# Loading the values by head pair, planning VectorE's and GpSimd's shared port, and filling TensorE's planned gaps in the opening with unread products

## The chip, the cores and the metric

The kernel runs on one core of a Trainium2 chip. The metric is the time of one execution on the device in microseconds; of several runs the median counts. Of the engines, TensorE (PE in the profile) multiplies, VectorE (DVE), ScalarE (ACT) and GpSimd (POOL) do the rest, and SyncE (SP) issues most of the transfers from the chip's memory.

## What is computed

Attention in a causal band of 64 positions for 8 batches of 8 heads (576 positions of 64 numbers), then a feed-forward layer on the 4608 tokens:

```python
scores = matmul(q, k.T) / 8; scores = where((rel >= 0) & (rel < 64), scores, -1e9)
attn = exp(scores - max); attn = attn / (sum(attn) + 1e-9)
x = matmul(attn, v)               # 4608 x 512, the heads side by side
h = x @ w_in                      # 512 x 2048
g = maximum(h, 0) + alpha * minimum(h, 0)
out = g @ w_out                   # 2048 x 512
```

All of it is in float32. The weights come as 64-bit floats, which the kernel turns into two parts itself.

## The kernel before

**Tiles and blocks.** The tokens are cut into 36 tiles of 128 (`t`), four tiles make a block (nine blocks), and the 2048 hidden features are cut into 16 groups of 128 (`f`). For each tile, `attend` loads q, k and v, multiplies scores (`score`, L366), adds the mask and takes the row's extreme on DVE (L382), the exponential on ACT (L388), the reciprocal of the sum on DVE (L399, L400), scales on POOL (L404), transposes the weights, and multiplies with v (`value`, L457). Tiles 0 to 7 are transposed on PE (`turn`, L421, and a copy `put`, L426 or L428), the others on DVE (L442). The result x is kept in a high part (`xh`, ACT, L461) and a low part (`xl`, DVE, L464), so that three products of a faster kind, high with high, low with high and high with low, stand for one in full float32.

**The feed-forward layer.** A `cell` is one block and one `f`: 12 products for h (L497), a slope on ACT (L503) and a maximum on DVE (L506), the high part `gh` on ACT (L511), the low part `gl` on POOL or, in block 0, on POOL or DVE (L515), and 12 products into the output (L530). The first four `f` of block 0 are done in two halves, tiles 0 and 1, then 2 and 3, with 256 columns instead of 512.

**The weights.** All 32 pieces (16 of w_in, 16 of w_out, in turn) are loaded into three `raw` buffers and converted once, by `weights`, while blocks 0 and 1 run: `two` (ACT or DVE, L260, L262), `shift` (DVE, L267, L270), `low` (ACT, L275), `val` (DVE, L279), the sum (POOL, L283), the high part `win_h` or `wout_h` (ACT, L298) and the low part `win_l` or `wout_l` (POOL or DVE, L302).

**The order.** All steps go into a `Plan` with their engines, a hold time and a latency each, written by hand in microseconds, with buffers taken and given and with due times. `order` (L73) walks through them like a list scheduler: it picks the step that can begin first on an engine, and among those within 0.12 us the one that is due first; where a step names two engines it takes the better. The sorted start times then give the order in which instructions are issued, once, when the program is built. On the chip, each engine runs its own instructions in that order and waits for what they need. PSUM's eight banks are split: 0 to 3 are kind `o` (the output sums of a block; before those begin, the first two tiles' scores and transposes and the first weights' `two`), 4 to 7 kind `bank`. A transposed weight tile lies in `pt`; the DVE path relies on zeros in the parts that it does not write, so a second such tile is set to zero by POOL (`birth`, L600).

**Loads.** q and k are one DMA each a tile. v of a tile lies as 128 rows (two overlapping stretches of 64 positions, each with the next) and is loaded in two DMAs of 64 partitions each (L346). For tiles 0 and 1 the second is issued from ACT's queue, all else from SP's. At most eight loads are in flight in the plan.

Of the kernel before, what the change touches and what calls it, by code (L numbers as in the profile page):

```python
# [24 lines left out]
FLIGHT = 8  # L25
SWITCH = 0.11
# [9 lines left out]
class Step:  # L36
    def __init__(self, engines, emit, after, behind, take, give, want, moved):
        self.engines, self.emit, self.after = engines, emit, [a for a in after if a is not None]
        self.behind, self.take, self.give, self.want, self.moved = behind, take, give, want, moved
        self.before, self.tiled, self.next = [], False, None  # L40
        self.start = self.end = None
        self.late = math.inf


class Plan:
# [5 lines left out]
    def step(self, engines, emit, after=(), behind=(), take=(), give=(), want=math.inf, moved=0.0):  # L51

        s = Step(engines, emit, after, list(behind), list(take), list(give), want, moved)
        for a in s.after + s.behind:
            a.before.append(s)
        self.steps.append(s)
        return s
# [13 lines left out]
    def order(self):  # L73
        self.deadlines()
        free = {PE: 0.0, DVE: 0.0, ACT: 0.8, POOL: 3.6, SP: 0.8}
# [4 lines left out]
        while ready:  # L80
            best = None
            picks = {}
            for s in ready:
# [11 lines left out]
                for e, (hold, lat) in s.engines.items():  # L95
                    picks.setdefault(e, []).append((max(t0, free[e]), s, e))
# [8 lines left out]
            while s:  # L105
# [6 lines left out]
                free[e] = t + hold  # L112
                s.end = t + lat
# [24 lines left out]
        return sorted(done, key=lambda s: s.start)  # L138
# [16 lines left out]
def banded_attention_then_prelu_ffn(  # L155
# [58 lines left out]
    def weight(name, f):  # L214
# [6 lines left out]
    stock = dict(bank=[4, 5, 6, 7], o=[0, 1, 2, 3], q=["q0", "q1"], k=["k0", "k1"], v=["v0"], w=["w0", "w1"],  # L221
                 pt=["pt0"], new=[], g=["g0", "g1"], gh=["gh0", "gh1", "gh2"], gl=["gl0", "gl1"],
# [5 lines left out]
    plan = Plan(stock)  # L228
    step = plan.step
# [11 lines left out]
    def weights(c):  # L241
# [58 lines left out]
        def rest(e):  # L300
# [13 lines left out]
        s7 = step({POOL: (1.22, 1.28), DVE: (1.15, 1.22)}, rest, [s6], prior[1:] if prior[0] else [],  # L314
                  take=late("_l"), give=[val])
# [6 lines left out]
    def attend(t, by_pe, want, loads_behind=(), behind=(), last=None):  # L322
# [3 lines left out]
        wb, pb = Buffer("w", 2 if by_pe else 1), Buffer("pt", 1)  # L326
# [3 lines left out]
        def load_q(e):  # L330
            d["q"] = room(qb, [P, 2, 2 * P], F32, f"q_{t}")
            (nc.scalar if e == ACT else nc.sync).dma_start(
                d["q"], qT[:, :, t].rearrange("(y x) d h q -> (x d) y (h q)", x=2))

        def load_k(_):
# [3 lines left out]
        loads = [step({SP: (0.62, 0.62)}, load_q, (), loads_behind, take=[qb], moved=0.75),  # L339
                 step({SP: (0.62, 0.62)}, load_k, (), loads_behind, take=[kb], moved=1.05)]  # L340
        lv = []
        for u in range(2):
            def load_v(e, u=u):
                if u == 0:
                    d["v"] = room(vb, [P, NP, 2, P], F32, f"v_{t}")
                (nc.scalar if e == ACT else nc.sync).dma_start(  # L346
                    d["v"][u * W:(u + 1) * W].rearrange("w c b d -> w c (b d)"),
                    vN[:, :, 2 * t + u:2 * t + u + 2].rearrange("c w b d -> w c (b d)"))
            lv.append(step({ACT if t < 2 and u else SP: (0.62, 0.62)}, load_v, (), [*loads_behind, *lv[:1]],
                           take=[vb] if u == 0 else [], moved=0.8 if t < 2 else 1.2))  # L350
# [18 lines left out]
        cold = 1.0 + 0.9 * (t < 2)  # L369
# [5 lines left out]
        for u in range(2):  # L375
            some = []
            for e in range(NP):
                g = u * NP + e

                def mask(_, u=u, e=e, g=g):  # L380
                    m = masks[:, 1 if (t * P + u * W) % seq == 0 else 0, :]
                    nc.vector.tensor_tensor_reduce(  # L382
                        out=d["w"][:, g, :], in0=d["s"][e % 2][:, u, e // 2], in1=m, op0=ALU.add, op1=ALU.min,
# [11 lines left out]
        def norm(u0, u1, after):  # L395
# [11 lines left out]
            r = step({DVE: (0.33, 0.4)}, recip, after)  # L407
# [3 lines left out]
        if by_pe:  # L411
            for u in range(2):
# [17 lines left out]
                tr = step({PE: (0.37 * cold, 0.5 * cold)}, turn, [sc] + ready[-1:], take=[tb] + [pb] * (u == 0), give=[wb])  # L430
# [245 lines left out]
```

## Time and profile before

| | before |
|---|---|
| median of 3 runs | 920.72 us (919.67 to 922.1) |
| profiled execution | 924.34 us, span 922.3 us |
| mean granted clock of TensorE | 0.996 |
| PE busy | 894.2 us, 97% |
| DVE, ACT, POOL busy | 446.5, 382.9, 316.0 us |
| read, written | 59.25 MB, 9.44 MB |

The span goes from the first to the last instruction of the core; the execution's own time lies 2.04 us above it. A row of the timeline has the start and the duration in microseconds, the engine, the line, the operation, what is written from what is read, the number of instructions run together, and in brackets how long the engine stood idle before and what ended that. Rows by operation have busy time, mean in ns, and idle time before with its releasers. Rows of stretches have, after the stretch and its length, the busy time of PE, PE's weight loads, DVE, ACT and POOL with the number of instructions, then the granted clock as a share of full speed, the share of the DMA engines, and GB/s. Numbers at names in the program's order are buffer numbers. Lines of the new kernel are higher than those of the old by 22 to 48, as the code has grown.

### The profile page before, as it was taken

What the parts mean: (1) busy time and instruction counts of PE and PEld (TensorE: products, weight loads), DVE (VectorE), ACT (ScalarE), POOL (GpSimd) and SP (SyncE); (2) the same over time, 40 slices, a digit from 0 to 9 for tenths busy, and PEclk for the clock granted to TensorE, in tenths of its full rate; (3) what the DMA queues carried; (4) which work ended last, traced back from release to release, by engine and by line L of the source; (5) the groups of instructions that cost most, each with busy time, mean ns of one, the idle gap of its engine ahead of it and who ended that gap; (6) DMA issues with size and microseconds to landing.
All of it is one profiled execution on the core that took longest, in us unless ns stands there. A gap on an engine that the chain in (4) does not pass through costs nothing.

```text
span 922.3 us, 15273 instructions
## 1 busy us (share of the span) xinstructions
PE 894.2 (97%) x5873; PEld 729.2 (79%) x5873; DVE 446.5 (48%) x1315; ACT 382.9 (42%) x1019; POOL 316.0 (34%) x244
## 2 busy tenths in 40 slices
PE   4799899999999999999999999999999999999998
PEld 3687678888888888888888888888888888888886
DVE  4889893744544445444544444445444444422111
ACT  4877784333433333333433343334333433322222
POOL 3677673322333223322233322333223322322221
PEclk9899999999999999999999999999999999999999
DMA  9476544011221123111211131113211221001001
GB/s 249 144 238 217 183 143 150 23 52 52 91 60 52 52 52 99 52 52 51 86 40 37 42 98 52 52 53 98 52 52 52 63 87 52 1 1 46 1 1 46
DMA packets 55209, 69.68 MB, mean 76 GB/s; under 512 B 3408, under 2 KB 48480, under 8 KB 55136
## 3 DMA queue, kind: packets, MB, share of 16 engines
q1 hardware_dynamic: 54560, 68.17, 25.1%
q8 instruction: 46, 0.75, 0.4%
q10 hardware_dynamic: 576, 0.53, 0.3%
q14 instruction: 27, 0.22, 0.1%
HBM read 59.25 MB, written 9.44 MB: 74 GB/s over the span
## 4 chain that ended last, share of the span: by engine, by line
PE 87%; DMA 4%; DVE 3%; ACT 2%; POOL 2%; issue 1%; SPq 0%; POOLq 0%; ACTq 0%; DVEq 0%
PE h L497 41%; PE o L530 39%; PE av L457 4%; PE s L366 3%; DMA raw<-w_out 2%; DMA raw<-w_in 1%; DMA q<-qT 1%; DMA v<-vN 1%; DVE val L279 1%; POOL val L283 1%; POOL wout_l L302 0%; DVE win_l L302 0%; ACT w L388 0%; POOL gl L515 0%; PE t L421 0%
## 5 line engine op out<-in xcount | busy, mean ns | idle before, releaser
L515 POOL TENSOR_TENSOR gl<-g,gh 128x512 fp32r<-128x512 f32 (+1 forms) x139 | 178.9, 1287 | 427.5 <-ACT gh L511 425.8
L506 DVE SCALAR_TENSOR_TENSOR g<-h,s_sb,g 128x512 f32<-128x512 f32 (+1 forms) x148 | 108.8, 735 | 293.8 <-ACT g L503 293.7
L503 ACT ACTIVATE g<-h,sa_sb 128x512 f32<-128x512 f32 (+1 forms) x148 | 100.2, 677 | 332.0 <-PE h L497 329.3
L530 PE MATMUL o<-wout_h,gh 128*128 128x512 f32 x576 | 226.8, 394 | 0.2 <-ACT gh L511 0.2
L530 PE MATMUL o<-wout_l,gh 128*128 128x512 f32 x576 | 226.2, 393 | 0.0
L497 PE MATMUL h<-xh,win_h 128*128 128x512 f32 (+1 forms) x592 | 160.8, 393 | 2.7 <-DVE val L279 2.7
L442 DVE STREAM_TRANSPOSE pt<-w 32x256 f32<-32x256 f32 x336 | 146.6, 436 | 30.9 <-POOL w L404 26.0
L530 PE MATMUL o<-wout_h,gl 128*128 128x512 f32 x576 | 160.7, 392 | 0.4 <-POOL gl L515 0.4
L497 PE MATMUL h<-xl,win_h 128*128 128x512 f32 (+1 forms) x592 | 156.1, 385 | 0.0
L497 PE MATMUL h<-xh,win_l 128*128 128x512 f32 (+1 forms) x592 | 155.6, 385 | 0.0
L388 ACT ACTIVATE w<-w,nm 128x128 f32<-128x128 f32 x288 | 112.1, 392 | 63.0 <-DVE nm L382 62.9
L511 ACT CAST gh<-g 128x512 fp32r<-128x512 f32 (+1 forms) x148 | 90.1, 609 | 111.3 <-DVE g L506 111.3
L497 PEld LDWEIGHTS h<-xl,win_h 128*128 128x128 f32 x592 | 109.9, 189 | 23.0
L530 PEld LDWEIGHTS o<-wout_h,gl 128*128 128x128 f32 x576 | 108.2, 188 | 25.0 <-POOL gl L515 0.8
L497 PEld LDWEIGHTS h<-xh,win_h 128*128 128x128 f32 x592 | 107.1, 189 | 26.4 <-ACT two L260 2.4
L497 PEld LDWEIGHTS h<-xh,win_l 128*128 128x128 f32 x592 | 110.0, 189 | 22.5
L530 PEld LDWEIGHTS o<-wout_h,gh 128*128 128x128 f32 x576 | 108.2, 188 | 24.3 <-ACT gh L511 0.6
L530 PEld LDWEIGHTS o<-wout_l,gh 128*128 128x128 f32 x576 | 108.2, 188 | 23.3
L404 POOL TENSOR_TENSOR w<-w,rc 128x1024 f32<-128x1024 f32 (+1 forms) x44 | 70.7, 1608 | 152.9 <-DVE rc L400 147.7
L382 DVE CUSTOM_DVE_ANT_0 w<-s,masks 128x128 f32<-128x128 f32 x288 | 63.9, 286 | 67.7 <-PE s L366 67.7
L388 ACT ACTIVATION_READ_ACCUMULATOR w<-w,nm 128x1 f32 x288 | 54.3, 189 | 0.0
L366 PE MATMUL s<-k,q 64*64 64x128 f32 x1152 | 43.1, 288 | 8.7 <-DMA q<-qT 6.1
(46 smaller groups left out, 458.6 us busy)
## 6 DMA issues: line engine op xcount, KB each, us to landing
v<-vN SPq DMA_DIRECT2D x70, 256.0 KB, 5.1
k<-kT SPq DMA_DIRECT2D x36, 384.0 KB, 3.9
q<-qT SPq DMA_DIRECT2D x36, 256.0 KB, 4.9
out<-os SPq DMA_DIRECT2D x36, 256.0 KB, 2.3
raw<-w_in SPq DMA_DIRECT2D x16, 512.0 KB, 4.4
raw<-w_out SPq DMA_DIRECT2D x16, 512.0 KB, 4.1
v<-vN ACTq DMA_DIRECT2D x2, 256.0 KB, 8.0
alpha_sb<-alpha ACTq DMA_DIRECT2D x1, 8.0 KB, 3.3
```

The source lines that it names most:

```text
L366: nc.tensor.matmul(d["s"][x][h * W:(h + 1) * W, u, y], q[r, y, h, u * W:(u + 1) * W], k[r, y, u:u + 2, h, :], start=True, stop=True)
L382: nc.vector.tensor_tensor_reduce(out=d["w"][:, g, :], in0=d["s"][e % 2][:, u, e // 2], in1=m, op0=ALU.add, op1=ALU.min, scale=-SCALE, scal ...
L388: nc.scalar.activation(w, w, AF.Exp, scale=-1.0, bias=d["nm"][:, g:g + 1], accum_out=d["sm"][:, g:g + 1])
L404: nc.gpsimd.tensor_tensor(out=w, in0=w, in1=d["rc"][:, g].unsqueeze(2).broadcast_to(list(w.shape)), op=ALU.mult)
L442: nc.vector.transpose(d["pt"][ks, :, r], d["w"][r, :, ks])
L457: nc.tensor.matmul(av[r, e, u * W:(u + 1) * W], d["v"][:, e, u, r], d["pt"][:, u * NP + e, h * W:(h + 1) * W], start=True, stop=True)
L497: nc.tensor.matmul(ph[:, :nt], weight(wt, f)[:, c * P:(c + 1) * P], xt[:, c, xs], start=(k == 0), stop=(k == 3 * NP - 1))
L503: nc.scalar.activation(d["g"], d["h"][:, :nt], AF.Copy, scale=sa_sb[:, f:f + 1])
L506: nc.vector.scalar_tensor_tensor(out=d["g"], in0=d["h"][:, :nt], scalar=s_sb[:, f:f + 1], in1=d["g"], op0=ALU.mult, op1=ALU.max)
L511: nc.scalar.copy(d["gh"], d["g"])
L515: (nc.gpsimd if e == POOL else nc.vector).tensor_tensor(out=d["gl"], in0=d["g"], in1=d["gh"].bitcast(F32), op=ALU.subtract)
L530: nc.tensor.matmul(po[t][0], gt[:, i * P:(i + 1) * P], weight(wt, f), start=(f == 0 and k == 0), stop=(f == NF - 1 and k == 2))
```

## The change

Four things change at once, and with them the order of the instructions through the opening and blocks 0 and 1.

- For tiles 0 to 7, v is loaded by head pair: four DMAs of 128 partitions and 128 KB each instead of two of 64 partitions and 256 KB, and all from SP. The rows of v then stand with the two halves of the band in turn, so the mask step writes its columns in that order too, with a step of two. As tile `pt0` is now filled in that other order, it gets a kind of its own (`mix`), and POOL sets it to zero (`clean`) before the DVE path uses it.
- The plan has a port that DVE and POOL share: a POOL step keeps it for its hold time, and a DVE step marked `port` (the reciprocals, the low parts of weights, `gl`) waits for it and keeps POOL off. The holds of such DVE steps are lower: 0.59 instead of 1.15 us for weights, 0.15 a tile instead of POOL's price for `gl`.
- `fill` puts a product of the identity with itself, 128 by 128, into a bank that nothing reads, wherever PE is free for more than 0.4 us in the plan between 3.6 and 28 us (`WARM`). That bank, 3, joins kind `o` only at 29 us. There are 38 such products in the built order.
- Some holds in the plan are lower: PE's steps count as slow for the first tile's scores alone, loads on SP as 0.5 instead of 0.62 us.

```diff
+WARM = 28.0
...
-        free = {PE: 0.0, DVE: 0.0, ACT: 0.8, POOL: 3.6, SP: 0.8}
+        free = {PE: 0.0, DVE: 0.0, ACT: 0.8, POOL: 3.6, SP: 0.8, (DVE, "port"): 3.6, (POOL, "port"): 0.0}
...
-                    picks.setdefault(e, []).append((max(t0, free[e]), s, e))
+                    t = max(t0, free[e])
+                    if e == POOL or s.port and e == DVE:
+                        t = max(t, free[e, "port"])
+                    picks.setdefault(e, []).append((t, s, e))
...
+                if e == POOL or s.port and e == DVE:
+                    free[DVE if e == POOL else POOL, "port"] = t + hold
...
-        return sorted(done, key=lambda s: s.start)
+        return sorted(done + self.fill(done), key=lambda s: s.start)
+
+    def fill(self, done):
+
+        some, t = [], 3.6
+        for s in sorted((s for s in done if s.engine == PE), key=lambda s: s.start):
+            while t + 0.4 < min(s.start, WARM):
+                some.append(Step({PE: (0.22, 0.22)}, self.idle, (), (), (), (), math.inf, 0.0, False))
+                some[-1].start, some[-1].end, some[-1].engine = t, t + 0.22, PE
+                t += 0.22
+            t = max(t, s.start + s.engines[PE][0])
+        return some
...
-    stock = dict(bank=[4, 5, 6, 7], o=[0, 1, 2, 3], q=["q0", "q1"], k=["k0", "k1"], v=["v0"], w=["w0", "w1"],
-                 pt=["pt0"], new=[], g=["g0", "g1"], gh=["gh0", "gh1", "gh2"], gl=["gl0", "gl1"],
+    stock = dict(bank=[4, 5, 6, 7], o=[0, 1, 2], q=["q0", "q1"], k=["k0", "k1"], v=["v0"], w=["w0", "w1"],
+                 mix=["pt0"], clean=[], pt=[], new=[], g=["g0", "g1"], gh=["gh0", "gh1", "gh2"], gl=["gl0", "gl1"],
...
+    plan.stock["o"].append((WARM + 1.0, 3))
+    spare = ps.tile([P, P], F32, tag="b3", name="spare")
+    plan.idle = lambda _: nc.tensor.matmul(spare, ident, ident, start=True, stop=True)
...
-        s7 = step({POOL: (1.22, 1.28), DVE: (1.15, 1.22)}, rest, [s6], prior[1:] if prior[0] else [],
-                  take=late("_l"), give=[val])
+        s7 = step({POOL: (1.22, 1.28), DVE: (0.59, 0.68)}, rest, [s6], prior[1:] if prior[0] else [],
+                  take=late("_l"), give=[val], port=True)
...
+        if by_pe:
+
+            for e in range(NP):
+                def load_v(_, e=e):
+                    if e == 0:
+                        d["v"] = room(vb, [P, NP, 2, P], F32, f"v_{t}")
+                    src = vN[e, :, 2 * t:2 * t + 2].rearrange("w b d -> w (b d)")
+                    src = bass.AP(src.tensor, src.offset, [list(src.ap[0]), [P, 2], list(src.ap[1])])
+                    nc.sync.dma_start(d["v"][:, e].rearrange("p b d -> p (b d)"), src)
+
+                lv.append(step({SP: (0.5, 0.5)}, load_v, (), [*loads_behind, *lv[:1]],
+                               take=[vb] if e == 0 else [], moved=0.38))
...
-        cold = 1.0 + 0.9 * (t < 2)
+        cold = 1.0 + 0.9 * (t < 1)
...
+                    w, s = d["w"][:, g, :], d["s"][e % 2][:, u, e // 2]
+                    if by_pe:
+                        w = w.rearrange("p (w b) -> p b w", b=2)
+                        s, m = (x.rearrange("p (b w) -> p b w", b=2) for x in (s, m))
...
-            r = step({DVE: (0.33, 0.4)}, recip, after)
+            r = step({DVE: (0.33, 0.4)}, recip, after, port=True)
...
-        s4 = step({POOL: (hold[4], lat[4]), DVE: (hold[4], lat[4])} if ts[0] < NBLK else {POOL: (hold[4], lat[4])},
-                  rest, [s3], take=[glb], give=[gb])
+        s4 = step({POOL: (hold[4], lat[4]), DVE: (0.15 * n, 0.15 * n + 0.1)} if ts[0] < NBLK else {POOL: (hold[4], lat[4])},
+                  rest, [s3], take=[glb], give=[gb], port=True)
...
+    old = Buffer("clean", 1, "pt")
+
+    def clean(_):
+        nc.gpsimd.memset(pts[old.at], 0.0)
+
+    step({POOL: (0.9, 0.95)}, clean, take=[old], give=[old])
```

More of the change, by code (lines that the diff above doesn't have):

```diff
@@ L36, with __init__ @@
 class Step:
-    def __init__(self, engines, emit, after, behind, take, give, want, moved):
+    def __init__(self, engines, emit, after, behind, take, give, want, moved, port):
         self.engines, self.emit, self.after = engines, emit, [a for a in after if a is not None]
         self.behind, self.take, self.give, self.want, self.moved = behind, take, give, want, moved
+        self.port = port
         self.before, self.tiled, self.next = [], False, None
@@ L49, in __init__, with step @@
             self.stock[kind] = [(0.0, p) for p in places]
-    def step(self, engines, emit, after=(), behind=(), take=(), give=(), want=math.inf, moved=0.0):
-        s = Step(engines, emit, after, list(behind), list(take), list(give), want, moved)
+    def step(self, engines, emit, after=(), behind=(), take=(), give=(), want=math.inf, moved=0.0, port=False):
+        s = Step(engines, emit, after, list(behind), list(take), list(give), want, moved, port)
         for a in s.after + s.behind:
@@ L337, in load_k, with load_v @@
             nc.sync.dma_start(d["k"], kT[:, :, 2 * t:2 * t + 3].rearrange("(y x) d b h w -> (x d) y (b h w)", x=2))
[L339 to L340 removed]
+        loads = [step({SP: (0.5, 0.5)}, load_q, (), loads_behind, take=[qb], moved=0.75),
+                 step({SP: (0.5, 0.5)}, load_k, (), loads_behind, take=[kb], moved=1.05)]
         lv = []
[L342 to L350, printed above, removed]
+        if by_pe:
[8 more added lines that the diff above has]
+                               take=[vb] if e == 0 else [], moved=0.38))
+        else:
+            for u in range(2):
+                def load_v(_, u=u):
+                    if u == 0:
+                        d["v"] = room(vb, [P, NP, 2, P], F32, f"v_{t}")
+                    nc.sync.dma_start(
+                        d["v"][u * W:(u + 1) * W].rearrange("w c b d -> w c (b d)"),
+                        vN[:, :, 2 * t + u:2 * t + u + 2].rearrange("c w b d -> w c (b d)"))
+                lv.append(step({SP: (0.62, 0.62)}, load_v, (), [*loads_behind, *lv[:1]],
+                               take=[vb] if u == 0 else [], moved=1.2))
         banks = [Buffer("o" if early else "bank", NP) for _ in range(2)]
@@ L465, in x_low @@
             d.clear()
-        va = step({PE: (1.08 * cold, 1.2 * cold)}, value, lv + ready, take=[ab], give=[vb, pb])
+        va = step({PE: (1.08, 1.2)}, value, lv + ready, take=[ab], give=[vb, pb])
         va.tiled = True
```

9 lines of the change are left out of this document (5 added, 4 removed).

## The prediction

> **What bounds the kernel now.** I read the stages first, then what the TensorE (PE) waits for, then the opening row by row. Four stretches of the span, with PE's busy time first, then weight loads, DVE, ACT and POOL, granted clock, DMA share and rate:
>
> ```profile
> 0.00:31.09 31.09, 14.64 (x213) 11.69 (x214) 18.21 (x93) 17.69 (x66) 13.53 (x22) 0.99 0.93 239
> 31.09:44.51 13.42, 12.38 (x113) 10.78 (x113) 9.22 (x23) 10.56 (x28) 8.80 (x9) 0.78 0.34 115
> 44.51:149.00 104.49, 98.44 (x685) 80.01 (x686) 87.44 (x190) 76.14 (x179) 76.68 (x59) 1.00 0.57 177
> 149.00:922.30 773.30, 768.69 (x4865) 626.74 (x4863) 331.59 (x1013) 278.51 (x749) 216.95 (x156) 1.00 0.19 55
> ```
>
> From 149 us on PE is busy 768.7 of 773.3 us: the rest of the program is a wall of matmuls, and an earlier start of it ends the program earlier by the same amount. The order of the instructions from there on is unchanged. So all that the change can do lies in the first 149 us. In them PE idles 16.45 us (31.09 less 14.64), then 1.04, then 6.05, and runs some products slowly. The rows of PE in the opening:
>
> ```profile
> 6.74 1.99 PE L366 MATMUL s<-k,q 64*64 64x128 f32 x32 [2.20 <-DMA q<-qT]
> 11.74 1.98 PE L366 MATMUL s<-k,q 64*64 64x128 f32 x32 [3.01 <-DMA q<-qT]
> 25.49 1.10 PE L366 MATMUL s<-k,q 64*64 64x128 f32 x32
> 26.53 1.15 PE L457 MATMUL av<-pt,v 128*64 128x64 f32 x32
> 27.61 0.66 PE L421 MATMUL t<-ident,w 128*128 128x128 f32 x4
> 31.09 1.09 PE L421 MATMUL t<-ident,w 128*128 128x128 f32 x4 [2.82 <-DVE xl L464]
> 31.83 1.20 PE L497 MATMUL h<-xh,win_h 128*128 128x256 f32 x4
> 34.67 1.98 PE L457 MATMUL av<-pt,v 128*64 128x64 f32 x32
> 37.22 0.72 PE L497 MATMUL h<-xh,win_h 128*128 128x256 f32 x4
> 44.51 0.71 PE L497 MATMUL h<-xh,win_h 128*128 128x256 f32 x4 [0.72 <-DVE val L279]
> ```
>
> The same 32 score products take 1.99 us at 6.74 and 1.10 us at 25.49, and the same 32 value products 1.15 us at 26.53 and 1.98 us at 34.67: PE runs at half speed early, at full speed around 25 to 28, and at half speed again after the 2.8 us without work before 31.09. The granted clock shows the second fall:
>
> ```profile
> 31.00:32.00 1.00, 0.91 (x5) 0.94 (x6) 1.00 (x6) 0.72 (x4) 0.83 (x1) 0.50 0.78 242
> 36.00:38.00 2.00, 2.00 (x23) 1.88 (x21) 1.32 (x4) 1.31 (x3) 2.00 (x2) 0.73 0.00 0
> ```
>
> (The early half speed is in the durations alone; the clock column of that time says 1.00.) From 31.83 to about 37 that costs 2.7 us: the first hidden product of 12 takes 2.84 us to 34.67, against some 1.44 us for one from 37.22 on, the value products 0.8 us, the transposes 0.4 us.
>
> **The chain to the first hidden product.** It needs xl of tile 1, which needs xh of tile 1, an ACT copy. These are ACT's rows on that way, and two DMAs of the chain that ended last:
>
> ```profile
> 1.29 7.23 DMA v<-vN
> 9.60 9.79 DMA raw<-w_out
> 19.41 0.67 ACT L275 ACTIVATE low<-raw 128x512 int32<-128x512 uint32 x1 [1.48 <-DMA raw<-w_out]
> 21.81 0.40 ACT L388 ACTIVATE w<-w,nm 128x128 f32<-128x128 f32 x1 [1.72 <-DVE nm L382]
> 26.32 0.62 ACT L298 CAST win_h<-val 128x512 fp32r<-128x512 f32 x1
> 26.84 0.69 ACT L275 ACTIVATE low<-raw 128x512 int32<-128x512 uint32 x1
> 29.51 0.56 ACT L461 CAST xh<-av 128x512 fp32r<-128x512 f32 x1
> ```
>
> On ACT, around that copy (v, raw: loads; low, wout_h, win_h: weights; w: the softmax; xh: the high half of the attention's output), before:
>
> ```order
> L298 CAST win_h<-val_283 128x512
> L275 ACTIVATE low_356<-raw_177 128x512
> L298 CAST wout_h<-val_325 128x512
> L388 ACTIVATE w_328,sm_330<-w_328,nm_329 128x128 x2
> L461 CAST xh<-av_359 128x4x128
> ```
>
> and now:
>
> ```order
> L320 CAST win_h<-val_266 128x512
> L502 CAST xh<-av_383 128x4x128
> L467 COPY pt_92<-t_0_409 128x512
> L429 ACTIVATE w_354,sm_356<-w_354,nm_355 128x128 x4
> L297 ACTIVATE low_447<-raw_224 128x512
> ```
>
> The copy of tile 1 moved up past one weight step, a wait for POOL and two exponentials. It began at 29.51 and can begin when win_h ends, at the 26.84 of the row behind it: **2.7 us** earlier, if the value products are there (PE had them at 27.61, before its long wait, and now has them as early relative to ACT).
>
> **When that stretch of ACT begins.** SP's loads in the opening, before (two more halves of v stood on ACT's queue):
>
> ```order
> L332 DMA q_102<-qT 128x2x256
> L346 DMA v_104<-vN 64x4x256
> L251 DMA raw_107<-w_in 128x4x256
> L337 DMA k_109<-kT 128x2x384
> L332 DMA q_117<-qT 128x2x256
> L346 DMA v_141<-vN 64x4x256
> L251 DMA raw_143<-w_out 128x1024
> ```
>
> and now:
>
> ```order
> L355 DMA q_103<-qT 128x2x256
> L373 DMA v_105<-vN 128x1x256 x4
> L273 DMA raw_119<-w_in 128x4x256
> L360 DMA k_143<-kT 128x2x384
> L355 DMA q_145<-qT 128x2x256
> L373 DMA v_147<-vN 128x1x256 x4
> L360 DMA k_170<-kT 128x2x384
> L273 DMA raw_200<-w_out 128x1024
> ```
>
> The first two tiles' k and q no longer share the engines with v, so the scores start earlier; but ACT now runs two weight steps on the first w_out before the exponentials of tile 2, so that load decides. One more k stands ahead of it. Sizes, and two microseconds of the opening that show the rate:
>
> ```profile
> v<-vN SPq DMA_DIRECT2D x70, 256.0 KB, 5.1
> k<-kT SPq DMA_DIRECT2D x36, 384.0 KB, 3.9
> 10.00:11.00 1.00, 0.00 (x0) 0.00 (x0) 0.68 (x8) 1.00 (x7) 0.00 (x0) 1.00 1.12 194
> 18.00:19.00 1.00, 1.00 (x12) 0.67 (x14) 0.33 (x1) 0.00 (x0) 0.92 (x1) 1.00 1.02 382
> ```
>
> 384 KB at the 239 GB/s of the opening cost 1.6 us. Against that, the engines are full (share over 1) at 194 GB/s in one microsecond and at 382 in another, so some transfers are dear; if the halves of v to 64 partitions are those, the 1 MB of v ahead of w_out goes from 5.4 us to 2.7 as transfers to 128 partitions. Bounds for the landing: 21.0 (no gain, 19.39 plus 1.6) and 18.3 (all of it); I take 18.6, near the second, since the DMA of v on its own queue, 7.2 us for 256 KB, is the slowest of the first loads. [...]
> Two weight steps (0.67 us each by the row at 19.41, some 0.6 apart) put the first exponential at 19.8 instead of 21.81: **2.0 us** (bounds -0.4 and 2.3). One set of transposes that stood ahead of the first hidden product now stands behind it: 0.4 us of work less done. Head start at the first hidden product: 2.7 + 2.0 - 0.4 = **4.3 us**, at about 27.1.
>
> **The idle products.** On PE around the first hidden product, now (spare: products of the identity that nothing reads; they wait for nothing):
>
> ```order
> L498 MATMUL av_383<-pt_92,v_147 64x64 x16
> L462 MATMUL t_0_409<-ident,w_269 128x128 x4
> L250 MATMUL spare<-ident 128x128 x4
> L538 MATMUL h_0_427<-xh,win_h 128x256 x4
> L538 MATMUL h_0_427<-xl,win_h 128x256 x4
> L538 MATMUL h_0_427<-xh,win_l 128x256 x4
> L462 MATMUL t_1_451<-ident,w_269 128x128 x4
> L250 MATMUL spare<-ident 128x128 x2
> ```
>
> There are 38 of them in all, each about a quarter of a set of transposes, so 0.28 us slow or 0.16 fast, 6.1 to 10.6 us in total; all but the last 10 stand where PE waits for loads, whose 16.45 idle us cover them. If that cover is gone, the ten in a row ahead of tile 0's transposes cost up to 2.8 us. With them PE is at work from about 19 to 27 without a gap of 2 us, so I take the hidden product at full speed. [...] If a gap that the plan did not foresee, from a late load, comes where no spare product stands, the 2.7 us are paid as now; that lies within the next step's end of 44.0.
>
> **What gives it back.** From there POOL sets the pace. The rows by operation (busy time and mean; for two of L302 shortest, median and longest), with what the next two parts need of ACT and DVE:
>
> ```profile
> L283 POOL TENSOR_TENSOR val<-val,low 128x512 int32<-128x512 int32 x32 | 44.4, 1397 | 6.7 <-DVE val L279 4.0 <-DVE rc L399 2.0 <-ACT low L275 0.7
> L404 POOL TENSOR_TENSOR w<-w,rc 128x512 f32<-128x512 f32 x16 | 17.5, 1099 | 20.2 <-DVE rc L400 15.0 <-ACT w L388 2.7 <-ACT pt L426 1.5
> L515 POOL TENSOR_TENSOR gl<-g,gh 128x256 fp32r<-128x256 f32 x3 | 2.8, 929 | 0.3 <-ACT gh L511 0.2
> L302 POOL TENSOR_TENSOR wout_l<-val,wout_h x10: 1267/1294/1302, 29.3 to 138.8; 128x512 fp32r<-128x512 f32 x10
> L302 DVE TENSOR_TENSOR win_l<-val,win_h x10: 682/1244/1802, 27.0 to 136.6; 128x512 fp32r<-128x512 f32 x10
> L302 DVE TENSOR_TENSOR win_l<-val,win_h 128x512 fp32r<-128x512 f32 x10 | 12.5, 1248 | 0.9 <-ACT win_h L298 0.6
> L302 DVE TENSOR_TENSOR wout_l<-val,wout_h 128x512 fp32r<-128x512 f32 x6 | 5.3, 888 | 0.9 <-ACT wout_h L298 0.9
> L464 DVE TENSOR_TENSOR xl<-av,xh 128x512 fp32r<-128x512 f32 x36 | 24.8, 690 | 6.5 <-ACT xh L461 6.5
> L426 ACT COPY pt<-t 128x512 f32<-128x512 f32 x11 | 6.4, 581 | 1.5 <-PE t L421 1.4
> L515 DVE TENSOR_TENSOR gl<-g,gh 128x256 fp32r<-128x256 f32 x5 | 3.8, 752 | 0.5 <-ACT gh L511 0.5
> L515 DVE TENSOR_TENSOR gl<-g,gh 128x512 fp32r<-128x512 f32 x4 | 5.2, 1300 | 0.0
> ```
>
> On POOL, where tile 3's second half of the softmax (w_328, now w_354) is scaled, before:
>
> ```order
> L404 TENSOR_TENSOR w_328<-w_328,rc_331 128x512
> L302 TENSOR_TENSOR win_l<-val_385,win_h 128x512
> L404 TENSOR_TENSOR w_328<-w_328,rc_331 128x512
> L283 TENSOR_TENSOR val_468<-val_468,low_472 128x512
> L283 TENSOR_TENSOR val_497<-val_497,low_490 128x512
> ```
>
> and now:
>
> ```order
> L445 TENSOR_TENSOR w_354<-w_354,rc_357 128x512
> L324 TENSOR_TENSOR wout_l<-val_424,wout_h 128x512
> L556 TENSOR_TENSOR gl_0_517<-g_0_490,gh_0_506 128x256
> L324 TENSOR_TENSOR win_l<-val_441,win_h 128x512
> L305 TENSOR_TENSOR val_523<-val_523,low_515 128x512
> L305 TENSOR_TENSOR val_537<-val_537,low_520 128x512
> L445 TENSOR_TENSOR w_354<-w_354,rc_357 128x512
> ```
>
> The scaling that tile 3 waits for moved behind four more steps. Step by step: hidden product from 27.1 to 28.5; transposes, copy, value products, xh of tile 2 and the cast wout_h, 0.4 + 0.6 + 1.15 + 0.56 + 0.62, to 31.9, a little later by ACT's queue, 32.1; POOL's 1.29 + 0.93 + 1.29 + 2 x 1.40 + 1.10 = 7.4 to 39.5; then transposes, copy, value products, xh and xl of tile 3, 0.5 + 0.6 + 1.15 + 0.56 + 0.69 = 3.5, with up to a microsecond for what stands ahead of xl on DVE: 43.0 to 44.0, taken 43.5. There the hidden products of tiles 2 and 3 begin; before, the same work was done at 44.51. So **1.0 us** of the 4.3 is left, the fast clock included.
>
> **From 44.5 to 149.** PE idles 6.05 us here, for DVE and for weights. The order gives DVE 19 instead of 16 low halves of weights and 7 instead of 4 wide gl, 3 instead of 5 narrow ones. POOL is rid of 6 wide ones at 1.29 and takes on 2 narrow ones at 0.93, 5.9 us off its 76.7. DVE gains 6 wide operations and loses 2 narrow ones at 0.75; a wide one takes 0.68 us at the shortest and about 1.25 to 1.30 where it meets POOL, so DVE gains 2.6 to 6.2 us on 87.4. The plan now keeps such operations clear of POOL's; if it succeeds, the 20 old wide ones, 12.5 + 5.3 + 5.2 = 23.0 us, give back up to 23.0 - 20 x 0.68 = 9.4 us. I take half of that, 4.7, and the middle of the other, 4.4: DVE's load stays as it is and POOL's falls. Of PE's 6.05 idle us I take a little under half off, as one of the two engines that it waits for gets lighter: **2.7 us** (bounds 0 and 6).
>
> Sum: 1.0 + 2.7 = 3.7 us. The profiled execution took 924.34 us for a span of 922.3; less 3.7 that is 920.6, and on the median of the runs shown, 920.72, 3.6 us under it, **917.0 us**.
>
> **The rivals.**
> *All given back.* POOL's late scaling eats the head start whole (the 44.0 end and w_out at 21.0), and the idle 6.05 us stay, since weights arrive through three raw buffers at a pace that the port does not set. For it: the DMA at 9.60, on the chain for 9.8 us. Result 919.5 to 921: no change. Chance 0.32.
> *DVE overloaded, slower.* The plan's DVE prices hold only if actual times match planned ones; with POOL busy 73% of 44 to 149, six more operations at 1.25 to 1.30 us, less the two narrow ones, add 6.2 us to an engine busy 84%. If two thirds reach PE and the rest of the head start is lost, 4.1 us: 925. It decides where the mean of DVE's wide low halves stays over 1.1 us. Chance 0.22. [...]
> *Loads faster still.* All early loads near 382 GB/s: the 4352 KB up to w_out take 11.7 us from about 2 us on, w_out lands before 16, ACT's own work on tile 1 then bounds the start, and 2.5 us more survive: 914.5. Chance 0.12.
> *The forecast*, 917.0 with its own range of 914 to 919, has 0.34.
>
> **How the numbers follow.** A measurement here tells about 0.3%, 2.8 us, from no change. Faster: the forecast and the fast loads, 0.46. Same: 0.32. Slower: 0.22. The range runs from 912 (head start kept, no idle left: 4.3 + 6 less some) to 925.
>
> **What would show it.** Right: the first hidden product near 27 at full speed, w_out's landing before 19, tile 3's transposes late near 40, PE's idle time in the 100 us after that under 4 us, DVE's low halves under 1.0 us in the mean. Wrong: the granted clock at 0.5 after 28, w_out after 20.5, or idle time over 6 us between the second pair's hidden products and the second block.

## The result, and the profile after

The change made the kernel slower: 929.16 us in the median of 4 runs (927.05 to 930.54) against 920.64 (919.67 to 922.1), a ratio of 1.0096 with a 95% interval of 1.0075 to 1.0117. Timed a second time it was 929.64 against 919.28, 1.0118 (1.0104 to 1.0133). The forecast was 917.0.

The profiled execution of the changed kernel took 927.05 us, the fastest of its four; that of the kernel before took 924.34, 3.7 above its median. So the two profiles differ by 3.0 us of span where the medians differ by 8.5. A second profile of the changed kernel, taken at its median (`after_again` below, 929.59 us), has 5.5 us more span than that of the kernel before, and the rest of the 8.5 lies in the latter's 3.7. The stretches of the changed kernel: up to the first hidden product, to the third, to the second block's first, and the rest; PE's busy time stands behind the length, then weight loads, DVE, ACT, POOL, granted clock, DMA share and rate:

```profile
0.00:25.47 25.47, 20.01 (x277) 17.41 (x277) 15.42 (x83) 16.59 (x62) 10.40 (x19) 1.00 0.82 270
25.47:42.90 17.43, 13.50 (x124) 11.10 (x125) 13.84 (x32) 12.10 (x34) 14.95 (x14) 0.91 0.39 124
42.90:150.83 107.93, 99.02 (x685) 79.44 (x684) 86.06 (x194) 74.44 (x177) 64.28 (x53) 1.00 0.52 170
150.83:925.30 774.47, 770.29 (x4865) 627.04 (x4863) 331.62 (x1013) 278.59 (x749) 216.98 (x156) 1.00 0.19 55
```

The first hidden product comes 6.4 us earlier than before (25.47 for 31.83), the third 1.6 us earlier (42.90 for 44.51), and the second block's first 1.9 us later (150.83 for 148.92; 153.35 in the second profile). From there on little differs: 774.5 us, before 773.4. (At 44.51 the kernel before began the first pair's third product and the second pair's first at 46.01; now the second pair's first is itself the third. The prediction called both the second pair's.)

PE's rows in the opening, of the changed kernel:

```profile
5.61 1.99 PE L403 MATMUL s<-k,q 64*64 64x128 f32 x32
7.53 2.80 PE L250 MATMUL spare<-ident 128*128 128x128 f32 x16
10.26 1.10 PE L403 MATMUL s<-k,q 64*64 64x128 f32 x32
25.47 0.74 PE L538 MATMUL h<-xh,win_h 128*128 128x256 f32 x4 [0.47 <-DVE xl L505]
37.63 0.66 PE L462 MATMUL t<-ident,w 128*128 128x128 f32 x4 [2.58 <-POOL w L445]
42.90 0.80 PE L538 MATMUL h<-xh,win_h 128*128 128x256 f32 x4
```

The second tile's scores take 1.10 us, where before they took 1.98 and came 1.5 us later: loads and idle products do what they were put in for. At 37.63 PE waits for the scaling on POOL, as the prediction said. What was lost lies behind 42.90. These are all of PE's waits there, each in brackets with what ended it:

```profile
58.82 1.20 PE L538 MATMUL h<-xh,win_h 128*128 128x512 f32 x4 [1.07 <-DVE g L547]
67.15 1.19 PE L538 MATMUL h<-xh,win_h 128*128 128x512 f32 x4 [0.57 <-DVE xl L505]
81.93 1.10 PE L403 MATMUL s<-k,q 64*64 64x128 f32 x32 [2.18 <-DVE val L301]
91.39 0.63 PE L462 MATMUL t<-ident,w 128*128 128x128 f32 x4 [2.24 <-DVE pt L469]
104.97 1.20 PE L538 MATMUL h<-xh,win_h 128*128 128x512 f32 x4 [0.47 <-DVE val L301]
119.90 0.63 PE L462 MATMUL t<-ident,w 128*128 128x128 f32 x4 [2.39 <-DVE val L301]
```

They add up to 8.9 us, which is the whole of PE's idle time in the stretch (107.93 less 99.02); before it was 6.05. All six end with DVE. Yet the low halves on DVE, whose stalls were to shrink, did get cheaper. In this kernel's trace the twelve wide ones with no POOL operation beside them take 0.68 or 0.69 us each, the seven that begin 0.29 us or more before one ends take 0.84 to 1.80. The groups (count, busy time and mean in ns of one):

```profile
L324 DVE TENSOR_TENSOR wout_l<-val,wout_h 128x512 fp32r<-128x512 f32 x12 | 10.6, 881 | 1.6 <-ACT wout_h L320 1.5
L556 DVE TENSOR_TENSOR gl<-g,gh 128x512 fp32r<-128x512 f32 x7 | 6.1, 870 | 2.1 <-PE t L462 0.9 <-ACT gh L552 0.7
L324 DVE TENSOR_TENSOR win_l<-val,win_h 128x512 fp32r<-128x512 f32 x7 | 5.8, 824 | 0.1
L556 DVE TENSOR_TENSOR gl<-g,gh 128x256 fp32r<-128x256 f32 x3 | 2.4, 806 | 0.0
```

Means of 0.82 to 0.88 us for the wide ones, before 0.89 to 1.30. DVE and POOL are both lighter in this stretch (86.06 and 64.28 us; before 87.44 and 76.68), though it is 3.5 us longer. So PE does not wait because an engine has too much to do. One of the waits from near by, the rows of DVE ahead of the one that ends at 91.39:

```profile
87.94 0.66 DVE L324 TENSOR_TENSOR win_l<-val,win_h 128x512 fp32r<-128x512 f32 x1
88.52 1.53 DVE L324 TENSOR_TENSOR wout_l<-val,wout_h 128x512 fp32r<-128x512 f32 x1
89.97 0.67 DVE L301 SCALAR_TENSOR_TENSOR val<-raw,two 128x512 int32<-128x512 int32 x1
90.57 0.68 DVE L469 COPY pt<-t 128x512 f32<-128x512 f32 x1
```

PE finished the first transposes at 89.15; the copy that the second ones wait for stands on DVE behind a low half and a weight step. DVE ran the weight step at 89.97 with the copy waiting since 89.15, and PE ran nothing in the meantime: both keep to their written order, and 2.24 us go. Here it is a matter of which instruction stands where.

### The profile page after: what moved, and what is told of

Same layout as the page of the kernel before. It is cut to its first block, busy times and chain, and to the rows that moved or that the text cites. A ratio compares the mean times of both kernels' runs of the same rounds, so it can differ in the third digit from the quotient of the medians.

```text
span 925.3 us, 15456 instructions
## 1 busy us (share of the span) xinstructions
PE 902.8 (98%) x5949; PEld 735.0 (79%) x5949; DVE 446.9 (48%) x1320; ACT 381.7 (41%) x1018; POOL 306.6 (33%) x241
## 4 chain that ended last, share of the span: by engine, by line
PE 86%; DVE 4%; DMA 4%; ACT 2%; issue 1%; POOL 1%; SPq 0%; POOLq 0%; ACTq 0%; DVEq 0%
PE h L538 40%; PE o L571 39%; PE av L498 4%; PE s L403 3%; DMA raw<-w_in 3%; DMA raw<-w_out 1%; DVE val L301 1%; DVE two L284 1%; DVE w L423 1%; DVE two L289 0%; ACT w L429 0%; PE t L462 0%; POOL val L305 0%; DVE wout_l L324 0%; DVE two L292 0%
## 5 line engine op out<-in xcount | busy, mean ns | idle before, releaser
L556 POOL TENSOR_TENSOR gl<-g,gh 128x512 fp32r<-128x512 f32 (+1 forms) x138 | 175.1, 1269 | 421.4 <-ACT gh L552 421.4
L305 POOL TENSOR_TENSOR val<-val,low 128x512 int32<-128x512 int32 x32 | 41.5, 1303 | 17.6 <-DVE val L301 10.6
```

Source lines behind the costliest of these rows:

```text
L305: nc.gpsimd.tensor_tensor(out=d["val"], in0=d["val"], in1=d["tail"], op=ALU.add)
L556: (nc.gpsimd if e == POOL else nc.vector).tensor_tensor(out=d["gl"], in0=d["g"], in1=d["gh"].bitcast(F32), op=ALU.subtract)
```

## The experiments

Twelve kernels, in three lots; times are medians, and each lot has its own median of the kernel before. "First" and "block 1" are the starts of the first hidden product and of the second block's first, "idle" is PE's from the third hidden product to block 1, all from the profile.

| kernel | us | before | ratio (95%) | first | block 1 | idle |
|---|---|---|---|---|---|---|
| no_port | 921.52 | 918.98 | 1.0027 (1.0017 to 1.0038) | 24.73 | 145.29 | 6.3 |
| no_spare | 923.88 | 918.98 | 1.0042 (1.0028 to 1.0057) | 27.21 | 148.90 | 8.1 |
| v_only | 921.86 | 918.98 | 1.0024 (1.0011 to 1.0036) | 27.53 | 145.03 | 6.1 |
| port_only | 916.12 | 918.98 | 0.9964 (0.9951 to 0.9976) | 29.48 | 140.87 | 2.1 |
| v_same_order | 916.77 | 919.38 | 0.9967 (0.9951 to 0.9984) | 28.09 | 141.95 | 3.5 |
| kq62 | 916.35 | 919.38 | 0.9970 (0.9950 to 0.9989) | 23.16 | 139.79 | 3.0 |
| look06 | 925.28 | 919.38 | 1.0065 (1.0043 to 1.0086) | 30.42 | 148.60 | 6.1 |
| retuned | 915.36 | 919.38 | 0.9956 (0.9941 to 0.9971) | 26.99 | 138.81 | 2.9 |
| after_again | 929.64 | 919.28 | 1.0118 (1.0104 to 1.0133) | 25.28 | 153.35 | 10.0 |
| after_nofill | 931.82 | 919.28 | 1.0142 (1.0125 to 1.0159) | 27.90 | 155.86 | 10.5 |
| low_to_pool | 928.60 | 919.28 | 1.0102 (1.0086 to 1.0119) | 25.41 | 152.38 | 7.1 |
| before_retuned | 921.47 | 919.28 | 1.0023 (1.0006 to 1.0039) | 29.18 | 146.11 | 7.3 |

The theories of the first lot: A, planning the shared port puts the instructions in an order in which PE waits for DVE's queue; B, the loads by head pair cost the time; C, the idle products and their bank do.

**no_port.** The changed kernel without the planning of the port:

```diff
-                    if e == POOL or s.port and e == DVE:
-                        t = max(t, free[e, "port"])
...
-                if e == POOL or s.port and e == DVE:
-                    free[DVE if e == POOL else POOL, "port"] = t + hold
...
-        s7 = step({POOL: (1.22, 1.28), DVE: (0.59, 0.68)}, rest, [s6], prior[1:] if prior[0] else [],
+        s7 = step({POOL: (1.22, 1.28), DVE: (1.15, 1.22)}, rest, [s6], prior[1:] if prior[0] else [],
...
-        s4 = step({POOL: (hold[4], lat[4]), DVE: (0.15 * n, 0.15 * n + 0.1)} if ts[0] < NBLK else {POOL: (hold[4], lat[4])},
+        s4 = step({POOL: (hold[4], lat[4]), DVE: (hold[4], lat[4])} if ts[0] < NBLK else {POOL: (hold[4], lat[4])},
```

> The changed kernel with the planning of the shared port taken out (no port times, the low halves of weights and of gl at their old planned prices on DVE); loads by head pair and idle products stay. Theory A (the planned port times put DVE's and PE's instructions in an order in which PE waits for DVE's queue): PE's idle time between the second pair's hidden products and block 1 goes back to 6 us or less, and the time to 917 to 922 us, since the head start stays. Theory B (the loads by head pair set the order and the pace of the weights in that stretch): the idle time stays at 8 to 9 us and the time at 927 to 931. Theory C (the idle products and the bank that they hold): the same as B, 927 to 931.

921.52: most of the loss is gone, as A said, if with 6.3 us of idle time.

**no_spare.** The changed kernel without the idle products:

```diff
-        return sorted(done + self.fill(done), key=lambda s: s.start)
+        return sorted(done, key=lambda s: s.start)
...
-    stock = dict(bank=[4, 5, 6, 7], o=[0, 1, 2], q=["q0", "q1"], k=["k0", "k1"], v=["v0"], w=["w0", "w1"],
+    stock = dict(bank=[4, 5, 6, 7], o=[0, 1, 2, 3], q=["q0", "q1"], k=["k0", "k1"], v=["v0"], w=["w0", "w1"],
...
-        cold = 1.0 + 0.9 * (t < 1)
+        cold = 1.0 + 0.9 * (t < 2)
...
```

> The changed kernel without the idle products: the fourth bank of the outputs is free from the start, and the planned prices of tile 1's cold products are as before; loads by head pair and port planning stay. Theories A and B: as slow as the changed kernel or slower, 927 to 935, since the first hidden products run at half the clock again (up to 2.7 us). Theory C: 919 to 924, and PE's idle time from the second pair's hidden products to block 1 at 6 us or less.

923.88: faster too, inside C's range and outside A's and B's, though its idle time stays at 8.1.

**v_only.** Both edits at once, so that of the change the loads by head pair are left, with the lower planned price of a load on SP (0.5 for 0.62), which is in all three of these kernels.

> The kernel before with v loaded by head pair for the first eight tiles, all on SP's queue, and nothing else of the change: no port planning, no idle products. Theory A: the loads come earlier and nothing gives it back, 916 to 920. Theory B: slower than the kernel before, 925 to 930, with 8 to 9 us of idle time of PE between the second pair's hidden products and block 1. Theory C: as A.

921.86, 2.9 us over the kernel before: between B's range and A's.

**port_only.** The kernel before, with the port times and lower prices alone:

```diff
+                    t = max(t0, free[e])
+                    if e == POOL or s.port and e == DVE:
+                        t = max(t, free[e, "port"])
...
+                if e == POOL or s.port and e == DVE:
+                    free[DVE if e == POOL else POOL, "port"] = t + hold
...
-        s7 = step({POOL: (1.22, 1.28), DVE: (1.15, 1.22)}, rest, [s6], prior[1:] if prior[0] else [],
-                  take=late("_l"), give=[val])
+        s7 = step({POOL: (1.22, 1.28), DVE: (0.59, 0.68)}, rest, [s6], prior[1:] if prior[0] else [],
+                  take=late("_l"), give=[val], port=True)
...
```

> The kernel before with the planning of the shared port and its lower prices alone: v by halves, no idle products. Theory A: slower than the kernel before, 925 to 930, with DVE's wide low halves at 0.7 to 0.9 us in the mean and yet more idle time of PE in the stretch than 6.05 us. Theories B and C: 917 to 920.5, since DVE's stalls shrink and nothing else is changed.

916.12: faster than the kernel before, and under every range. A falls, since the planning of the port by itself gains; B can't explain why taking the idle products away helps; C can't explain v_only. No part that A, B or C names is the culprit: each removal gives 5 to 8 us back, and each also makes the planner choose anew. That gave theory D: the planner fits step after step greedily, so any changed price or duration gives another order, and where a step may run on two engines (low halves, `two`, copies) another choice of engine too; the constants were fitted to the order before, and the change drew a poor one. (The table of planned starts that some expectations speak of is the planner's own, worked out when the kernel is built; it is no measurement. Built from the kernels, it puts the second block at 133.3 us before the change and at 139.7 after it.)

**v_same_order.** To price the loads without a new order, the kernel before was kept instruction for instruction; its 16 half loads became 32 loads of a head pair, and the masks write the layout that goes with them:

```diff
...
+                for x in (2 * u, 2 * u + 1):
+                    src = vN[x, :, 2 * t:2 * t + 2].rearrange("w b d -> w (b d)")
+                    src = bass.AP(src.tensor, src.offset, [list(src.ap[0]), [P, 2], list(src.ap[1])])
+                    (nc.scalar if e == ACT else nc.sync).dma_start(d["v"][:, x].rearrange("p b d -> p (b d)"), src)
...
```

> The kernel before in its own order, instruction for instruction; only the 16 half loads of v for the first eight tiles are 32 loads of one head pair to all 128 partitions, two at each place (ACT still issues those of the first two tiles' second place), and the masks write their windows interleaved. Theory B (the loads by head pair themselves cost time in the stretch from 44 to 150 us): slower than the kernel before by 2 to 4 us, as the run with these loads and a new order was. New theory D (the loads are no dearer; any change of a planned price makes the planner, which fits the instructions greedily, choose another order, and the change drew a poor one where the constants had been fitted to the order before): not slower than before, 0 to 3 us faster, 915.5 to 919.5.

This kernel leaves out the clearing of a buffer of transposed weights between the two layouts, one POOL operation of 0.95 us; in the changed kernel POOL sat idle for 8.27 us ahead of it, so it is unlikely to matter. 916.77, 2.6 us faster than before: B falls. The rates of three stretches of 5 us in the opening, first of the kernel before, then of this one:

```profile
5.00:10.00 5.00, 1.99 (x32) 1.61 (x32) 1.34 (x13) 0.77 (x4) 0.00 (x0) 1.00 1.08 242
10.00:15.00 5.00, 1.98 (x32) 1.61 (x32) 1.88 (x19) 3.32 (x19) 0.49 (x1) 1.00 1.11 277
15.00:20.00 5.00, 3.52 (x36) 2.82 (x40) 3.77 (x16) 3.52 (x15) 2.63 (x3) 1.00 1.06 287
```

```profile
5.00:10.00 5.00, 2.91 (x51) 2.57 (x55) 2.00 (x18) 1.91 (x10) 0.00 (x0) 1.00 0.97 309
10.00:15.00 5.00, 2.25 (x25) 1.47 (x21) 3.72 (x25) 5.00 (x25) 2.08 (x2) 1.00 1.04 372
15.00:20.00 5.00, 5.00 (x72) 4.04 (x72) 4.58 (x24) 2.52 (x9) 3.32 (x3) 1.00 1.08 378
```

The last column rises from 242, 277 and 287 GB/s to 309, 372 and 378 with the DMA engines about as full (shares of 1.08, 1.11 and 1.06, then 0.97, 1.04 and 1.08), in the same order and for the same 69.68 MB. Whether the 128 partitions or the smaller size of a load does it, no run tells apart.

**kq62.** The changed kernel with one number of the planner set back:

```diff
-        loads = [step({SP: (0.5, 0.5)}, load_q, (), loads_behind, take=[qb], moved=0.75),
-                 step({SP: (0.5, 0.5)}, load_k, (), loads_behind, take=[kb], moved=1.05)]
+        loads = [step({SP: (0.62, 0.62)}, load_q, (), loads_behind, take=[qb], moved=0.75),
+                 step({SP: (0.62, 0.62)}, load_k, (), loads_behind, take=[kb], moved=1.05)]
```

> The changed kernel with one planned price set back: SP's issue of a k or q load at 0.62 us, as before the change, in place of 0.5. No instruction is added, taken away or changed; only the order that the planner chooses differs. The planner's own table puts the second block about 6 us earlier with it. Theory D: most of the loss goes, 918 to 923 us, and PE's idle time from the second pair's hidden products to block 1 is under 6 us. Theories A and B (the planning of the port, or the loads by head pair, costs the time): 927 to 931 as the changed kernel, since both are all there.

916.35, 13 us under the changed kernel and under D's range too. The work is the same, but not only the order is new, as the expectation has it: 35 idle products stand in it instead of 38, and 13 low halves of weights run on DVE instead of 19, the others on POOL. Its stretches and its waits of PE up to block 1 from the third hidden product, to be set against those of the changed kernel above:

```profile
0.00:23.16 23.16, 18.51 (x265) 15.78 (x265) 14.38 (x81) 15.83 (x60) 10.36 (x19) 1.00 0.89 295
23.16:37.49 14.33, 12.29 (x124) 10.80 (x125) 11.66 (x29) 10.97 (x31) 12.24 (x11) 0.88 0.44 143
37.49:139.79 102.30, 99.26 (x692) 80.42 (x691) 85.83 (x195) 76.65 (x181) 72.64 (x59) 1.00 0.57 181
```

```profile
46.07 0.71 PE L538 MATMUL h<-xh,win_h 128*128 128x256 f32 x4 [0.30 <-DVE val L301]
51.54 0.73 PE L538 MATMUL h<-xh,win_h 128*128 128x256 f32 x4 [0.55 <-DVE g L547]
75.01 1.10 PE L403 MATMUL s<-k,q 64*64 64x128 f32 x32 [0.66 <-DVE g L547]
77.45 1.16 PE L538 MATMUL h<-xh,win_h 128*128 128x512 f32 x4 [1.33 <-DVE val L301]
115.12 0.63 PE L462 MATMUL t<-ident,w 128*128 128x128 f32 x4 [0.17 <-DVE g L547]
```

The same work has 3.0 us of waits instead of 8.9. Of the 11.0 us between the two spans, 2.3 lie ahead of the first hidden product, 3.1 between it and the third, 5.6 behind. A and B, which had 927 to 931, fall with this run. Is it then the price of a load itself, or the other split between the engines? `retuned` below keeps the price of 0.5 and is the fastest. And `port_only`, with 20 low halves of weights on DVE, has 2.1 us of waits; over all these kernels the load does not go with the waits: `no_spare` has the least work on DVE in this stretch (84.20 us) and 8.1 us of waits, `v_same_order` has 88.48 and 3.5, and `retuned`, with the most on POOL (83.72 us), has 2.9.

**look06.** The other way round, the kernel before with one constant changed:

```diff
-LOOK = 0.12
+LOOK = 0.06
```

> The kernel before with the planner's tolerance LOOK at 0.06 in place of 0.12 (of the steps that could start within that of the first, the most urgent is taken). No work is changed, only the order; the planner's own table puts the second block about 5 us later with it. Theory D: slower than before by 3 to 8 us, 922 to 927. Theories A and B, for which the loss comes from what the change adds: within 2 us of the kernel before.

925.28, 5.9 us slower with nothing of the change in it. D holds on the other side too. How the time is lost differs: this kernel's waits in the stretch are those of the kernel before (6.1 us for 6.05), but after a wait of 1.90 us at 88.78 four hidden products took 1.91 us (at 90.48) and 1.86 (at 92.19), ahead of it 1.08 and 1.07, the granted clock of the stretch is 0.98 for 1.00, and PE is busy for 102.53 us for 98.44.

**retuned.** The changed kernel with constants fitted anew:

```diff
-LOOK = 0.12
+LOOK = 0.15
-FIRST, PACE, TURN, LONG = 20.0, 5.6, 112.0, 97.0
+FIRST, PACE, TURN, LONG = 24.0, 5.8, 112.0, 97.0
```

> The changed kernel with three constants of the planner fitted anew (LOOK 0.15, FIRST 24, PACE 5.8; they were 0.12, 20 and 5.6, as before the change), chosen by the planner's own table, which puts the second block 7.7 us earlier than in the changed kernel. All work of the change is there. Theory D: 914 to 920, that is the change's head start kept at least in part. Theories A and B: 925 to 931.

915.36, the fastest of all, 4.0 us under the kernel before and 14 under the changed one. Two groups of its low halves on DVE:

```profile
L324 DVE TENSOR_TENSOR wout_l<-val,wout_h 128x512 fp32r<-128x512 f32 x8 | 8.7, 1085 | 0.9 <-ACT wout_h L320 0.9
L556 DVE TENSOR_TENSOR gl<-g,gh 128x512 fp32r<-128x512 f32 x5 | 5.3, 1066 | 1.1 <-ACT gh L552 0.9
```

They stall more than in the changed kernel (1.09 and 1.07 us in the mean for 0.88 and 0.87), though fewer of them run on DVE, and it is the fastest kernel: the stalls beside POOL are not what decides.

**after_again and after_nofill.** The changed kernel again, and the same without issuing its idle products, all else in place:

```diff
-            s.emit(s.engine)
+            if s.emit != plan.idle:
+                s.emit(s.engine)
```

> The changed kernel as it is, timed on the same chip as the runs beside it: all theories 926 to 931.

> The changed kernel in its own order, but the 38 idle products are not issued; everything else, the bank kept from the outputs included, stands where it stood. Prediction's step (they keep TensorE at full speed, worth up to 2.7 us at the first hidden product): that product 1 to 3 us later, half-speed products before it. Theory D (what PE waits for from 45 to 120 us are places in the order, which the head start does not reach): the time within 1.5 us of the changed kernel all the same, 927 to 931. Rival (the head start carries through): 2 to 3 us slower, 930 to 934.

First hidden product and first product of block 1, of after_again and then of after_nofill:

```profile
25.28 0.74 PE L538 MATMUL h<-xh,win_h 128*128 128x256 f32 x4 [0.46 <-DVE xl L505]
153.35 0.86 PE L538 MATMUL h<-xh,win_h 128*128 128x512 f32 x3
```

```profile
27.90 0.74 PE L538 MATMUL h<-xh,win_h 128*128 128x256 f32 x4 [1.35 <-DVE xl L505]
155.86 0.86 PE L538 MATMUL h<-xh,win_h 128*128 128x512 f32 x3
```

Without idle products the first is 2.6 us later, block 1 is 2.5 us later, and the time is 2.2 us longer (four runs each, whose intervals against the kernel before overlap; the traces agree with it). The rival was right here and D's figure too small: in this fixed order the head start is passed on. So nothing that is fixed in time, such as a pace of loads, stands between; a pace that moves along with the head start isn't ruled out.

**low_to_pool.** Two low halves of the changed kernel moved from DVE to POOL, behind the scaling, the rest in its own order:

```diff
+            if c in (17, 28) and e == DVE:
+                kept.append(rest)
+                return
...
+                if u1 == 2 and kept:
+                    kept.pop()(POOL)
```

> The changed kernel in its own order but for two instructions: the two low halves that took 1.53 us on DVE, ahead of what PE's second transposes at 91.39 and its transposes at 119.90 waited for, run on POOL instead, right behind the scaling. Theory D, made local (PE waits there for the in-order queue of DVE): both waits, 2.24 and 2.39 us, shrink by 0.8 to 1.5 us each, block 1 starts 1.5 to 3 us earlier, 925.5 to 928. Rival (the pace of the weights stands behind them, and another wait follows): the waits shrink but the time stays within 1 us of the changed kernel.

The two waits in after_again, then what stands there in this kernel:

```profile
91.23 0.63 PE L462 MATMUL t<-ident,w 128*128 128x128 f32 x4 [2.22 <-DVE pt L469]
120.95 0.70 PE L462 MATMUL t<-ident,w 128*128 128x128 f32 x4 [3.24 <-DVE val L301]
```

```profile
91.39 0.63 PE L468 MATMUL t<-ident,w 128*128 128x128 f32 x4 [0.88 <-DVE pt L475]
118.39 0.63 PE L468 MATMUL t<-ident,w 128*128 128x128 f32 x4 [1.04 <-DVE val L302]
120.51 1.92 PE L544 MATMUL h<-xh,win_h 128*128 128x512 f32 x4 [1.49 <-DVE val L302]
```

Both waits shrink, by 1.3 and 2.2 us, and 1.0 us is left in the time, less than the runs can tell from nothing. At 91 PE comes later to the place, since the granted clock was 0.50 in 84 to 86 us (rows in the last section); behind 118 a new wait of 1.49 us follows, for a val that now waits for the low half on POOL. Over the stretch PE idles 2.9 us less (7.1 for 10.0) and is busy 2.0 us longer (102.32 for 100.33, at a mean clock of 0.97 for 0.98). Inconclusive in time: the waits are local to the queues, but most of the gain went into products at a fallen clock, and whether that fall is this order's or chance the runs don't show.

**before_retuned.** Constants of the kernel before fitted by the same rule:

```diff
-LOOK = 0.12
+LOOK = 0.05
-FIRST, PACE, TURN, LONG = 20.0, 5.6, 112.0, 97.0
+FIRST, PACE, TURN, LONG = 20.0, 6.0, 112.0, 97.0
-EARLY = (14.0, 18.0, 23.0, 28.0)
+EARLY = (14.0, 19.0, 25.0, 31.0)
```

> The kernel before with three constants of the planner fitted anew by the same rule and among as many tries as for the changed kernel (LOOK 0.05, PACE 6.0, EARLY 14, 19, 25, 31). Theory D with the change worth nothing: 914 to 917, as the changed kernel with its fitted constants (915.36). Theory D with the head start worth something in a good order: 917.5 to 920, that is 2.5 us or more behind it.

921.47, slower than both expectations and than the kernel before, though the planner's table preferred it by 0.6 us (132.7 for 133.3). The table had the sign right where it promised 5 us and more (kq62, look06, retuned), and not here. The five plans with the second block at 131.9 to 133.7 took 915.4 to 921.5 us, the three at 136.3 to 136.4 (no_port, no_spare, v_only) 921.5 to 923.9, the two at 138.6 and 139.7 (look06 and the changed kernel) 925.3 and 929.6. So three orders of the kernel before took 919.3 to 925.3 us, three of the changed one 915.4 to 929.6.

## Why the prediction was wrong

*The head start at the first hidden product*, forecast at 4.3 us: right in its mechanism and too small, 6.4 (25.47 for 31.83). ACT's first step on the first w_out began at 17.66, so the load was there sooner than the 18.6 taken, and the cast win_h began 2.8 us earlier (23.48 for 26.32), not 2.0. The copy behind it gained the 2.7 as said (23.99 for 29.51 in all). From the copy to the product 0.8 us fell away, where the sum took 0.4 off. In a fixed order the loads alone gain 2.6 us in time.

*The idle products*, full speed at the first hidden product: right (0.74 us for its first four products, before 1.20), and worth 2.2 us in the fixed order of the changed kernel. It does not hold to the third product: after the wait of 2.58 us at 37.63 the granted clock fell to 0.50, as the first two of three rows below show; that was one of the prediction's signs of being wrong.

*Given back by POOL's late scaling*: right in the wait, and in the time partly by luck. The third hidden product was forecast at 43.5 and came at 42.90; 1.6 us of lead were left for 1.0. But the scaling ended at 37.58, 1.9 us before the 39.5 taken, and what held PE last was not xl (done at 42.44) but six output products from 40.18 on, which the sum did not have and which ran at the fallen clock (0.50 in 41 to 43 us).

***From 44.5 to 149***: this step failed. "PE's 6.05 idle us ... a little under half off, as one of the two engines that it waits for gets lighter: 2.7 us", with bounds of 0 and 6. POOL did get lighter, by more than was said, DVE too, and PE's idle time rose to 8.9 (10.0 in the second profile). The step took waits for a share of the engines' load. They are places in an order; the whole order of that stretch was new, and in these kernels the load did not tell the waits. kq62 shows it: same work, DVE as busy (85.83 for 86.06), POOL busier (72.64 for 64.28), 3.0 us of waits. The bound of 0, that nothing could be lost here, had no reason behind it; look06 shows that the order can cost the kernel before 5.9 us by itself. And the new order could be read without a run: the changed kernel's own plan has the second block 6.3 us later than the plan before (139.7 for 133.3), which the prediction did not use.

*The sum* was made against a profiled execution 3.7 us above the median of its kernel. By the first profiles the change costs 3.0 us (2.9 more idle, 0.7 more busy time of PE up to block 1 and 1.1 behind it, less the lead of 1.6); by the medians 8.5.

*The rivals.* "DVE overloaded" came nearest in its time (925), by a mechanism that was not there: the means lie under the 1.1 us from which it was to decide, and DVE has less to do in that stretch. "Loads faster still" was half right, at the opening only. No rival said that the order itself was at stake.

What stays open: what the planning of the port is worth, since it can't be had without a new order; which of the places in an order decide, since low_to_pool mended two and gained 1.0 us; and whether the best order of the changed kernel beats the best of the kernel before, of which three each were tried. The parts that could be priced in a fixed order gain 2.6 and 2.2 us.

## What to carry to other kernels

Where a greedy planner sets the order, each changed price draws a new order, and between orders of the same work lay 14 us here; so hold the order fixed to price a part, and fit the planner's constants anew before judging the whole. Compare the planned starts of both kernels first: a difference of 5 us or more had the right sign each time here. Waits of an engine in an order written down are not a share of another engine's load: in these kernels neither a lighter engine nor shorter stalls went with shorter waits, and the prediction's range has to hold a poor order as well as a good one. Take the profiled execution's distance from its kernel's median into account before reading a difference of a few us from two profiles.

## What the runs showed of the hardware

The clock fell after shorter gaps than the 2.8 us of the prediction (1.96 and 1.90 us below), and not after each (2.18 and 3.24 us). The granted clock is the third column from the right: the changed kernel after the 2.58 us wait at 37.63, and after the 2.18 us wait at 81.93:

```profile
39.00:41.00 2.00, 2.00 (x34) 1.79 (x35) 1.28 (x3) 0.59 (x1) 1.73 (x2) 0.71 0.04 16
41.00:43.00 2.00, 2.00 (x6) 1.54 (x6) 2.00 (x4) 0.43 (x1) 1.27 (x1) 0.50 0.20 29
82.00:84.00 2.00, 2.00 (x37) 1.65 (x38) 2.00 (x6) 0.70 (x3) 2.00 (x3) 1.00 0.48 147
```

And low_to_pool, which waits 1.96 us at the same place (to 81.65):

```profile
82.00:84.00 2.00, 2.00 (x32) 1.58 (x25) 2.00 (x10) 0.69 (x3) 2.00 (x3) 0.78 0.67 203
84.00:86.00 2.00, 2.00 (x6) 1.52 (x6) 1.97 (x16) 2.00 (x12) 1.80 (x2) 0.50 0.66 189
```

After the gap of 1.96 us the clock went to 0.50, after that of 2.18 it stayed at 1.00, and in both falls shown it comes some 2.2 and 1.5 us after work is back (estimates from the shares of 0.71 and 0.78, taken as a step from 1.00 to 0.50). The widest pair is a wait of look06, after which four hidden products took 1.91 us for 1.08, and one of before_retuned, after which they took 0.64 us at half the width, as before it (the granted clock from 40.60 to 146.11 is 1.00):

```profile
88.78 0.66 PE L421 MATMUL t<-ident,w 128*128 128x128 f32 x4 [1.90 <-DVE val L279]
49.70 1.10 PE L366 MATMUL s<-k,q 64*64 64x128 f32 x32 [3.24 <-DVE g L506]
```

One order's time goes with it: of the 32 executions of the kernel before in the second lot, the seven with a mean granted clock of 0.999 or more have a median of 918.4 us, the ten with 0.996 or less 921.1.
